# Agent attention into a gated convolution: two of five shifted taps left to DMA, three copied by VectorE, and the score and value units gathered in five blocks per batch

## The chip, the cores and the metric

The kernel runs on one core of a Trainium2 chip. The core has five engines, each with its own queue of instructions worked off in order: TensorE (PE; its weight loads are shown as PEld), VectorE (DVE), ScalarE (ACT), GpSimd (POOL) and SyncE (SP), which here issues nearly all DMA transfers. They meet through semaphores. The metric is the device time of one execution in microseconds, as the median of several runs.

## The reference

There are four batches of 12800 rows with 128 columns. Forty-nine agents first gather the values by attention over the keys, and then hand them out by attention over the queries. The result x goes through a causal convolution of five taps, whose sigmoid gates x @ w_val, and through w_out.

```python
def sm(a, b):
    s = scale * (a @ b.transpose(0, 2, 1))
    s = s - s.max(-1, keepdims=True)
    e = np.exp(s)
    return e / (e.sum(-1, keepdims=True) + 1e-09)
agent_v = sm(agents, k) @ v
x = sm(q, agents) @ agent_v
...
for k in range(K):                      # K = 5, xp is x behind K - 1 rows of zeros
    gate_pre += conv_w[k][None, None, :] * xp[:, k:k + S, :]
gate = 1.0 / (1.0 + np.exp(-gate_pre))
out = gate * (x @ w_val) @ w_out
```

## The kernel before, in words

x is never formed. Since x is (query weights) @ agent_v, the convolution, w_val and agent_v are folded per batch into small matrices (`fold_weights`), and what the matmuls move is the transposed query weights: 49 agents on the partitions, rows of the sequence in the free dimension.

**Units and chunks.** Keys, values and queries come in units of 1280 rows, ten per batch and kind. A key unit (k) is a score matmul group (sc, 16 matmuls), a copy to ks and a maximum; a value unit (v) is two exponentials, a 32x32 block transpose on VectorE (eT) and ten small matmuls (av); a query unit (q) is a score group, a VectorE transpose (sT), a maximum, and the softmax over VectorE, GpSimd and ScalarE, which ends in the tile pt. The output is worked off in 100 chunks of 512 rows, 25 per batch: six gate matmuls, two value matmuls, tanh (th, ScalarE), h = (th + 1) * val (VectorE), hh (ScalarE, 16 bits), hl = h - hh (GpSimd), and, two chunks later, three output matmuls and the scaled copy ob. The gate and the value sums have one PSUM bank each, so h of a chunk has to have read val before the next chunk's value matmuls write it.

**Precision by doubled rows.** Query weights are split in two 16-bit halves, high and low. A transposed tile x1 has 128 partitions: 49 high rows, 49 low rows, and 30 high rows a second time, which meet the low halves of the folded weights. For the other 19 agents a second tile x2 holds the high rows of all five taps (20 rows for each, 100 in all), each shifted by its tap, so that one more gate matmul (L832) and one more value matmul (L859) do for them. pt is brought into x1 by a DMA transpose (L743, all units but the first four, which go over TensorE), and x2 is filled from x1 by five shifted DMA transfers per pair of units (`shifts`, L791), or per unit for the first four. All of these but two are in SyncE's queue, between loads and stores.

**Order.** `Plan` collects the steps with their engine, an assumed duration, and what they read and write, and `order()` places them by list scheduling: TensorE's steps keep the order in which they were added, the steps of the other engines go by the longest tail of work behind them. For a transfer it assumes the wire time and a landing of 1.4 us (`LAND`). The order in which units come between chunks is a list: the tuple `at` names ten chunks of a batch, and ahead of each stand its query unit and its key or value units. Keys of the next batch come first, then the key maxima (behind chunks 7 and 8), then the values, then the fold behind chunks 20 to 24.

```python
at = (0, 2, 5, 7, 10, 12, 15, 17, 20, 22)
...
    before[t0 + at[i]].append(("q", g // NU, g % NU))
    ...
    before[t0 + at[n // part]].append(("k", b + 1, u))
    ...
    before[t0 + at[AV0 + u // 2]].append(("v", b + 1, u))
```

Loads have eleven buffers and are issued in the order of use.

Of the kernel before, what the change touches and what calls it, by code (L numbers as in the profile page):

```python
# [9 lines left out]
F32 = mybir.dt.float32  # L10
# [3 lines left out]
ALU = mybir.AluOpType  # L14
AX = mybir.AxisListType
# [16 lines left out]
X2LO = 29  # L32
X2R = 20
# [18 lines left out]
T_AT = 7  # L52
HOP = 0.09
# [9 lines left out]
class Plan:  # L63
# [7 lines left out]
    def __init__(self):  # L71
        self.steps, self.urge = [], []
        self.wrote, self.read = {}, {}

    def add(self, engine, us, fn, reads=(), writes=(), moved=0.0, key=None, urge=0.0):
# [11 lines left out]
        self.urge.append(urge)  # L87

    def order(self):
# [32 lines left out]
        while done < n:  # L122
# [33 lines left out]
            if moved:  # L156
                wire = max(wire, when + 0.5) + moved
                end = max(wire, when + us) + LAND
                lanes = lanes[1:] + [end]
# [12 lines left out]
def tile_agent_attention_gated_conv(  # L172
# [11 lines left out]
    A = 49  # L184
    NU = N // UNIT
# [26 lines left out]
    qw = ring(3, [P, NBLK, A], F32, "qw")  # L212
# [52 lines left out]
    for t in wst_sb:  # L265
        nc.gpsimd.memset(t[:, TAPS + 1 :, :], 0.0)

# [6 lines left out]
    def weights():  # L274
# [4 lines left out]
        else:  # L279
# [51 lines left out]
            for fn in ops:  # L331
# [5 lines left out]
                out=cmax, in_=conv_sb, axis=AX.X, op=ALU.max, apply_absolute_value=True  # L337
# [41 lines left out]
    def key_scores(b, u):  # L379
# [13 lines left out]
        if not first:  # L393
# [5 lines left out]
                out=kmx[b % 2][:, u, :], in_=src, axis=AX.X, op=ALU.max  # L399
# [6 lines left out]
    def key_max(b):  # L406
# [6 lines left out]
                out=m2, in_=kmx[x].rearrange("p u j -> p j u"), axis=AX.X, op=ALU.max  # L413
# [9 lines left out]
        def spread():  # L423
            nc.vector.tensor_reduce(
                out=mrow, in_=p1[0:2, 0:P].rearrange("j (g a) -> j a g", g=G),
                axis=AX.X, op=ALU.max,
# [58 lines left out]
    def fold_weights(b):  # L485
# [19 lines left out]
        def normalise():  # L505
            dve.tensor_scalar_add(den, pt[:, 0:A], 1e-9)
            dve.reciprocal(out=den, in_=den)
            dve.tensor_tensor(out=avT, in0=pt[:, AP_ : AP_ + A], in1=den, op=ALU.mult)
# [11 lines left out]
        def gate_scale():  # L520
            dve.tensor_reduce(
                out=mx[:, 0:1], in_=avT, axis=AX.X, op=ALU.max, apply_absolute_value=True
# [18 lines left out]
        x2g = wst[:, TAPS + 1, 0 : TAPS * X2R].rearrange("p (k r) -> p k r", k=TAPS)  # L541
        x2v = wst[:, TAPS + 2, 0 : TAPS * X2R].rearrange("p (k r) -> p k r", k=TAPS)
        ghi = wst[:, 0:TAPS, 0:A]
        vhi = wst[:, TAPS, 0:A]
        off = NDUP - X2LO

# [6 lines left out]
        def val_weights():  # L553
            dve.tensor_reduce(
                out=mx[:, 1:2], in_=pv[:, 0:A], axis=AX.X, op=ALU.max,
# [8 lines left out]
            rest(wst[:, TAPS, 2 * A :], pv[:, 0:NDUP], 1, vhi[:, 0:NDUP])  # L564
            rest(x2v[:, HALO, off:], pv[:, NDUP:A], 1, vhi[:, NDUP:])
# [4 lines left out]
        def gate_rest():  # L570
            rest(wst[:, 0:TAPS, 2 * A :], gw[:, :, 0:NDUP], 0, ghi[:, :, 0:NDUP])
            rest(x2g[:, :, off:], gw[:, :, NDUP:], 0, ghi[:, :, NDUP:])
# [3 lines left out]
        add("dve", 1.2, val_weights, [at_v], [(*w_, "v"), "mxv"])  # L576
        add(
            "act", 0.4,
            lambda: nc.scalar.copy(out=wst[:, 0:TAPS, A : 2 * A], in_=ghi),
# [3 lines left out]
            "act", 0.22, lambda: nc.scalar.copy(out=wst[:, TAPS, A : 2 * A], in_=vhi),  # L583
            [(*w_, "v")], [(*w_, "e")],
        )
        add("dve", 0.7, gate_rest, ["gw", (*w_, "g")], [(*w_, "r")])
# [46 lines left out]
        def split():  # L633
            dve.tensor_reduce(
                out=oscale, in_=po[:, 0:P], axis=AX.X, op=ALU.max, apply_absolute_value=True
# [31 lines left out]
    def queries(b, u):  # L667
# [6 lines left out]
        sa = sT[:, :, 0:A]  # L674
# [4 lines left out]
            lambda: nc.vector.tensor_reduce(out=qmx[x], in_=sa, axis=AX.X, op=ALU.max),  # L679
# [5 lines left out]
                out=d, in0=sa, in1=qmx[x].unsqueeze(2).to_broadcast([P, NBLK, A]),  # L685
# [10 lines left out]
        def sums():  # L696
            nc.vector.tensor_reduce(out=sm, in_=e, axis=AX.X, op=ALU.add)
# [9 lines left out]
                out=w, in0=e, in1=r.unsqueeze(2).to_broadcast([P, NBLK, A]), op=ALU.mult  # L707
# [5 lines left out]
            "act", 0.58, lambda: nc.scalar.copy(out=pt[:, :, 0:A], in_=w),  # L713
# [5 lines left out]
                out=pt[:, :, 2 * A :], in0=w[:, :, 0:NDUP], scalar1=1.0, scalar2=0.0,  # L719
# [338 lines left out]
```

## Time and profile before

| what | value |
|---|---|
| median of 3 runs | 430.09 us (429.39 to 432.08) |
| the profiled execution | 431.22 us, span 429.4 us |
| granted TensorE clock, mean | 0.996 |
| TensorE busy | 402.9 us (94%) |
| VectorE, ScalarE, GpSimd busy | 297.0, 300.4, 224.3 us |
| DMA | 128.07 MB, mean 298 GB/s |

The profile is of one execution. A row of a group of instructions gives the line, the engine, the operation, what it writes and reads, a count, then the busy time and the mean ns of one, and the idle time ahead of it with what ended most of it. A row of waits gives who waited, for whom, the us in total, how often, and the longest. The chain of waits is followed back from the last instruction; its rows are the start, the length and the work. Matmuls are pipelined and the profile models their ends, so the spacing of their starts says more than their durations.

### The profile page before, as it was taken

The page shows a single profiled execution, that of the slowest core. Times are in us where ns is not written, and L with a number is a line of the kernel's source. Part 1 is how long each engine was busy: PE and PEld are TensorE (multiplying, and loading weights), DVE is VectorE, ACT ScalarE, POOL GpSimd, SP SyncE. Part 2 cuts the span into 40 slices and gives each one's busy share as a digit, 9 for nine tenths or more (in the row PEclk, how much of TensorE's full clock was granted, in tenths as well). Part 3 has the DMA queues.
Part 4 walks back from the last instruction along what each step waited for, and adds up shares of the span by engine and source line. Part 5 has one row for each costly group of instructions (what it writes and reads, how often), then busy time and mean ns, then how long its engine had stood idle before and what let it go on. Part 6 is the DMA issues. An engine that isn't in the chain of part 4 may idle for free.

```text
span 429.4 us, 8968 instructions
## 1 busy us (share of the span) xinstructions
PE 402.9 (94%) x3307; PEld 194.8 (45%) x3307; DVE 297.0 (69%) x555; ACT 300.4 (70%) x520; POOL 224.3 (52%) x239
## 2 busy tenths in 40 slices
PE   3978888999999999999999999999999999999995
PEld 1357333345565444444555544445555544434443
DVE  3776879886786877578666887678666787566231
ACT  1464536678976577778876676778876577777875
POOL 1002246564466665544557665553356466687553
PEclk9999989999999999999999999999999999999999
DMA  8999999999999999999999999999999999887743
GB/s 288 422 415 415 371 350 337 297 285 309 343 358 294 249 270 289 307 309 305 340 329 356 292 323 292 320 312 334 306 330 257 289 291 287 215 199 173 192 156 122
DMA packets 76158, 128.07 MB, mean 298 GB/s; under 512 B 51644, under 2 KB 51900, under 8 KB 76116
## 3 DMA queue, kind: packets, MB, share of 16 engines
q1 hardware_dynamic: 76056, 127.41, 96.0%
q8 instruction: 26, 0.43, 0.4%
q14 instruction: 16, 0.13, 0.1%
q10 hardware_dynamic: 60, 0.10, 0.1%
HBM read 79.25 MB, written 26.21 MB: 246 GB/s over the span
## 4 chain that ended last, share of the span: by engine, by line
PE 65%; DMA 13%; DVE 12%; ACT 5%; issue 3%; SPq 1%; POOL 1%; DVEq 0%; ACTq 0%; POOLq 0%
PE gate L828 20%; PE sc L363 13%; PE av L463 6%; PE gate L832 4%; PE val L855 4%; PE val L859 4%; PE out L898 4%; PE out L899 4%; PE out L900 4%; DMA ld<-qT 3%; DMA ld<-vP 3%; DVE h L868 2%; ACT e L455 2%; DMA ld<-kT 2%; DMA outT<-ob 2%
## 5 line engine op out<-in xcount | busy, mean ns | idle before, releaser
L879 POOL TENSOR_TENSOR hl<-h,hh 128x512 f16<-128x512 f32 (+1 forms) x101 | 117.0, 1160 | 121.3 <-ACT hh L874 113.7
L828 PE MATMUL gate<-x,stat 128*128 128x512 f16 (+1 forms) x500 | 124.4, 378 | 2.4 <-ACT th L841 2.3
L868 DVE SCALAR_TENSOR_TENSOR h<-th,val 128x512 f32<-128x512 f32 x100 | 67.7, 677 | 69.1 <-PE out L899 46.1
L363 PE MATMUL sc<-ld,ag_sb 128*32 128x320 f32 x1280 | 102.0, 452 | 10.0 <-DMA ld<-kT 8.0
L912 ACT ACTIVATE ob<-out,oscale 128x512 f32<-128x512 f32 x98 | 67.2, 686 | 23.5 <-PE out L900 17.4
L841 ACT ACTIVATE th<-gate,unscale 128x512 f32<-128x512 f32 x100 | 68.3, 683 | 19.7 <-PE gate L832 18.0
L828 PEld LDWEIGHTS <-stat 128*128 128x128 f16 x505 | 45.6, 97 | 66.4 <-issue 19.0
L874 ACT CAST hh<-h 128x512 f16<-128x512 f32 (+1 forms) x101 | 61.4, 608 | 13.1 <-DVE h L868 12.4
L684 POOL TENSOR_TENSOR qw<-sT,qmx 128x490 f32<-128x490 f32 x40 | 41.5, 1038 | 50.2 <-DVE qmx L679 50.1
L363 PEld LDWEIGHTS sc<-ld,ag_sb 128*32 128x32 f32 x1280 | 37.0, 112 | 62.8 <-issue 22.5
L463 PE MATMUL av<-ld,eT 128*64 128x129 f32 x800 | 49.5, 275 | 1.7 <-DMA ld<-vP 1.4
L389 ACT COPY ks<-sc 128x640 f32<-128x640 f32 x40 | 27.7, 691 | 32.7 <-PE sc L363 30.6
L463 PEld LDWEIGHTS av<-ld,eT 128*64 128x64 f32 x800 | 43.7, 136 | 11.7 <-issue 7.3
L726 POOL TENSOR_TENSOR pt<-qw,pt 128x490 f16<-128x490 f32 x40 | 44.7, 1119 | 3.8 <-ACT pt L713 3.1
L455 ACT ACTIVATE e<-ks,kbias 128x320 f32<-128x320 f32 x80 | 39.0, 553 | 6.1 <-DVE kbias L444 3.3
L373 DVE STREAM_TRANSPOSE eT<-e 128x640 f32<-128x640 f32 x40 | 33.6, 842 | 11.4 <-ACT e L455 5.9
L373 DVE STREAM_TRANSPOSE sT<-sc 128x640 f32<-128x640 f32 x40 | 33.3, 834 | 10.8 <-PE sc L363 10.6
L398 DVE TENSOR_REDUCE kmx<-ks 128x2 f32<-128x640 f32 x39 | 31.4, 817 | 11.8 <-ACT ks L389 11.8
L832 PE MATMUL gate<-x,stat 100*128 100x512 f16 x100 | 38.0, 380 | 0.8 <-DMA x<-x 0.8
L855 PE MATMUL val<-x,stat 128*128 128x512 f16 x100 | 37.8, 378 | 0.1
L859 PE MATMUL val<-x,stat 100*128 100x512 f16 x100 | 37.8, 378 | 0.0
L898 PE MATMUL out<-hh,wo 128*128 128x512 f16 x98 | 37.1, 379 | 0.0
(125 smaller groups left out, 392.1 us busy)
## 6 DMA issues: line engine op xcount, KB each, us to landing
ld<-vP SPq DMA_DIRECT2D x40, 645.0 KB
ld<-kT SPq DMA_DIRECT2D x40, 640.0 KB
ld<-qT SPq DMA_DIRECT2D x40, 640.0 KB
outT<-ob SPq DMA_DIRECT2D x48, 512.0 KB
x<-x SPq DMA_DIRECT2D x90, 100.0 KB
x<-x SPq DMA_DIRECT2D x18, 50.0 KB
outT<-ob SPq DMA_DIRECT2D x3, 256.0 KB
x<-pt SPq DMA_TRANSPOSE x36
```

The source lines that it names most:

```text
L363: nc.tensor.matmul(out=out[g * BLK : (g + 1) * BLK, j, 0:GT], lhsT=ag_sb[:, b, j * BLK : (j + 1) * BLK], rhs=src[:, g * GT : (g + 1) * GT] ...
L373: nc.vector.transpose(out=out.rearrange("p n (j i) -> p j n i", j=2), in_=in_.rearrange("p j (n i) -> p j n i", i=BLK),)
L463: nc.tensor.matmul(out=av[o : o + AP_, 0 : C + 1], lhsT=et[:, n, :], rhs=vt[:, n, :], start=(u == 0 and n < 2), stop=(u == NU - 1 and n >= ...
L828: nc.tensor.matmul(out=pg, lhsT=stat[:, k, :], rhs=x1[:, c : c + w], start=(k == 0), stop=False,)
L832: nc.tensor.matmul(out=pg, lhsT=stat[0 : TAPS * X2R, TAPS + 1, :], rhs=x2[0 : TAPS * X2R, o2 : o2 + w], start=False, stop=True,)
L841: lambda: nc.scalar.activation(out=th, in_=pg, func=AF.Tanh, scale=unscale[:, 0:1]),
L855: nc.tensor.matmul(out=pv, lhsT=stat[:, TAPS, :], rhs=x1[:, PAD + n0 : PAD + n0 + w], start=True, stop=False,)
L859: nc.tensor.matmul(out=pv, lhsT=stat[0 : TAPS * X2R, TAPS + 2, :], rhs=x2[0 : TAPS * X2R, o2 : o2 + w], start=False, stop=True,)
L868: lambda: nc.vector.scalar_tensor_tensor(out=h, in0=th, scalar=1.0, in1=pv, op0=ALU.add, op1=ALU.mult),
L874: "act", 0.16 + 0.42 * scale, lambda: nc.scalar.copy(out=hh, in_=h),
L879: lambda: nc.gpsimd.tensor_tensor(out=hl, in0=h, in1=hh, op=ALU.subtract),
L912: lambda: nc.scalar.activation(out=ob[:, o : o + w], in_=po, func=AF.Copy, scale=oscale),
```

## The change

Two things are changed. First, of the five shifted copies into x2, taps 0, 2 and 4 are now VectorE copies (`tensor_copy`, within SBUF, 16 bits) and taps 1 and 3 stay DMA transfers. The rows are laid out anew, so that the copies read and write from partitions that are multiples of 32: pt has two of the doubled rows ahead of the high rows (`A0 = 2`), the 19 rows that x2 needs begin at partition 32 of x1, and taps 0, 4 and 2 lie at partitions 0, 64 and 32 of x2. Tap 1 has its rows at 97, and tap 3 what is left, in two pieces (at 116 and 20). The unused rows of x2 are set to zero once, on GpSimd, and the matmuls over x2 read all 128 partitions. The agents are laid out with the two extra columns on the host, so that scores and the query softmax are 51 wide instead of 49 where they must be. The small operations that fill the low halves of the folded weights (`rest`) follow the new rows: three on the value side where two stood, six on the gate's where two stood. `Plan.add` has a new number, `spare`, which lets the plan count 2 us more for the landing of a DMA transpose.

Second, `at` names five chunks twice each: a block of two query and four key or value units ahead of chunks 0, 5, 10, 15 and 20.

```diff
+SPARE = 2
...
+X2_ROWS = (
+    ((0, 19, 0),),
+    ((0, 19, 97),),
+    ((0, 19, 32),),
+    ((0, 12, 116), (12, 7, 20)),
+    ((0, 19, 64),),
+)
...
+    for t in x2s:
+        nc.gpsimd.memset(t, 0.0)
...
-                [(*p_, n) for n in range(3)], [("x1", u)], 2.4,
+                [(*p_, n) for n in range(3)], [("x1", u)], 2.4, spare=SPARE,
...
         for k in range(TAPS):
             c = PAD - HALO + u0 * UNIT + k
-
-            q, e = (nc.scalar, "act") if g == 0 and k % 2 else (nc.sync, "dma")
-            add(
-                e, 0.75,
-                lambda k=k, c=c, q=q: q.dma_start(
-                    out=x2[k * X2R : (k + 1) * X2R, o : o + n * UNIT],
-                    in_=x1[X2LO : X2LO + X2R, c : c + n * UNIT],
-                ),
-                src, [("x2", s % 3, o + i * UNIT, k) for i in range(n)], 0.26 * n,
-            )
+            for i, m, r in X2_ROWS[k]:
+                out, in_ = x2[r : r + m, o : o + w], x1[REST + i : REST + i + m, c : c + w]
+                keys = [("x2", s % 3, o + j * UNIT, k, i) for j in range(n)]
+                if k % 2 == 0:
+                    add(
+                        "dve", 0.08 + 0.33 * n,
+                        lambda out=out, in_=in_: nc.vector.tensor_copy(out=out, in_=in_),
+                        src, keys,
+                    )
+                    continue
...
+                add(
+                    e, 0.75, lambda out=out, in_=in_, q=q: q.dma_start(out=out, in_=in_),
+                    src, keys, 0.013 * m * n,
+                )
...
-    at = (0, 2, 5, 7, 10, 12, 15, 17, 20, 22)
+    at = (0, 0, 5, 5, 10, 10, 15, 15, 20, 20)
```

What moves on TensorE, at chunk 35 (ten chunks into the second batch): its rows before, where L363 is a score unit, L463 a value unit, L828 the first gate matmul of a chunk and L900 the last output matmul; numbers behind names tell buffers apart.

```order
L900 MATMUL out<-hl_113,wo_123 128x512
L363 MATMUL sc_128<-ld_70,ag_sb 32x320 x8
L463 MATMUL av<-ld_71,eT_83 64x129 x10
L463 MATMUL av<-ld_61,eT_84 64x129 x10
L828 LDWEIGHTS stat_121
L828 MATMUL gate<-x_99,stat_121 128x512
...
L363 MATMUL sc_129<-ld_62,ag_sb 32x320 x8
L463 MATMUL av<-ld_63,eT_82 64x129 x10
L463 MATMUL av<-ld_64,eT_83 64x129 x10
```

The same place after; the lines have other numbers (L379 score, L479 value, L870 gate, L942 output).

```order
L942 MATMUL out<-hl_113,wo_123 128x512
L379 MATMUL sc_128<-ld_70,ag_sb 32x320 x8
L379 MATMUL sc_129<-ld_71,ag_sb 32x320 x8
L479 MATMUL av<-ld_61,eT_83 64x129 x10
L479 MATMUL av<-ld_62,eT_84 64x129 x10
L479 MATMUL av<-ld_63,eT_82 64x129 x10
L479 MATMUL av<-ld_64,eT_83 64x129 x10
L870 LDWEIGHTS stat_121
L870 MATMUL gate<-x_99,stat_121 128x512
```

Two score units and four value units now stand together ahead of chunk 35, and the block that stood ahead of chunk 37 is gone from there.

On VectorE, the rows before around the h of the chunks at the same place (h is L868, the transposes of value and query units are L373, the maximum over the agents L679).

```order
L868 SCALAR_TENSOR_TENSOR h_107<-th_104,val 128x512
L373 STREAM_TRANSPOSE sT_86<-sc_128 128x2x10x32
L679 TENSOR_REDUCE qmx_88<-sT_86 128x10
L373 STREAM_TRANSPOSE eT_84<-e_80 128x2x10x32
L373 STREAM_TRANSPOSE eT_82<-e_81 128x2x10x32
L373 STREAM_TRANSPOSE eT_83<-e_80 128x2x10x32
L868 SCALAR_TENSOR_TENSOR h_108<-th_105,val 128x512
L868 SCALAR_TENSOR_TENSOR h_106<-th_103,val 128x512
```

And after, with what each row waits for (L910 is h, L389 the transposes, L821 the new copies; DMAHW is a transfer's landing).

```order
L910 SCALAR_TENSOR_TENSOR h_107<-th_104,val 128x512 [waits Activation_49,Pool_49]
L389 STREAM_TRANSPOSE eT_82<-e_81 128x2x10x32 [waits DVE_49,PE_49]
L389 STREAM_TRANSPOSE sT_85<-sc_129 128x2x10x32 [waits Pool_49]
L389 STREAM_TRANSPOSE eT_83<-e_80 128x2x10x32 [waits DVE_49,PE_49,Activation_49]
L389 STREAM_TRANSPOSE eT_84<-e_81 128x2x10x32 [waits DVE_49,PE_49,Activation_49]
L389 STREAM_TRANSPOSE eT_82<-e_80 128x2x10x32 [waits DVE_49,PE_49,Activation_49]
L821 COPY x_102<-x_99 19x2560 [waits DMAHW5_49,DMAHW4_49]
L910 SCALAR_TENSOR_TENSOR h_108<-th_105,val 128x512 [waits PE_49,Activation_49]
L821 COPY x_102<-x_99 19x2560 x2
L910 SCALAR_TENSOR_TENSOR h_106<-th_103,val 128x512 [waits PE_49,Activation_49,Pool_49]
```

Three copies have come in around two h, and the first of them waits for the two DMA transposes of its pair of units; the h behind it is behind that wait as well.

More of the change, by code (lines that the diff above doesn't have):

```diff
@@ L87, in add @@
         self.urge.append(urge)
+        self.spare.append(spare)
     def order(self):
@@ L820, in gates @@
         xs = [("x1", u) for u in units] + [("x1b", u) for u in units]
-        x2k = [("x2", segs_[0] % 3, h, k) for h in halves for k in range(TAPS)]
+        x2k = [
+            ("x2", segs_[0] % 3, h, k, i) for h in halves for k in range(TAPS)
+            for i, _, _ in X2_ROWS[k]
+        ]
         st = [("stat", x, 0), ("stat", x, 1)]
@@ L832, in matmuls @@
             nc.tensor.matmul(
-                out=pg, lhsT=stat[0 : TAPS * X2R, TAPS + 1, :],
-                rhs=x2[0 : TAPS * X2R, o2 : o2 + w], start=False, stop=True,
+                out=pg, lhsT=stat[:, TAPS + 1, :], rhs=x2[:, o2 : o2 + w],
+                start=False, stop=True,
             )
@@ L859, in matmuls @@
             nc.tensor.matmul(
-                out=pv, lhsT=stat[0 : TAPS * X2R, TAPS + 2, :],
-                rhs=x2[0 : TAPS * X2R, o2 : o2 + w], start=False, stop=True,
+                out=pv, lhsT=stat[:, TAPS + 2, :], rhs=x2[:, o2 : o2 + w],
+                start=False, stop=True,
             )
```

100 lines of the change are left out of this document (61 added, 39 removed).

## The prediction

> **What bounds the kernel now.** The busy totals of the page come first, then the windows, which give every engine's busy time in each stage.
>
> ```profile
> PE 402.9 (94%) x3307; PEld 194.8 (45%) x3307; DVE 297.0 (69%) x555; ACT 300.4 (70%) x520; POOL 224.3 (52%) x239
> ```
>
> ```profile
> core 0: us, PE busy (x) PEld busy (x) DVE busy (x) ACT busy (x) POOL busy (x), PEclk, DMA share, GB/s
> 0.00:50.30 50.30, 37.28 (x483) 21.80 (x484) 32.66 (x74) 23.61 (x42) 6.62 (x17) 1.00 0.98 381
> 50.30:100.00 49.70, 45.28 (x379) 18.80 (x377) 42.01 (x78) 32.02 (x55) 27.02 (x30) 0.97 1.00 324
> 100.00:150.00 50.00, 49.21 (x442) 26.52 (x438) 37.13 (x69) 37.38 (x68) 30.96 (x32) 1.00 0.99 311
> 150.00:200.00 50.00, 49.91 (x402) 22.18 (x400) 36.64 (x67) 37.23 (x63) 25.77 (x28) 1.00 1.06 298
> 200.00:250.00 50.00, 48.90 (x424) 25.67 (x421) 36.61 (x69) 37.11 (x67) 30.36 (x32) 1.00 1.01 323
> 250.00:300.00 50.00, 49.96 (x405) 22.33 (x404) 36.54 (x67) 38.00 (x65) 26.29 (x27) 1.00 1.03 316
> 300.00:350.00 50.00, 48.73 (x399) 25.57 (x398) 35.91 (x66) 35.98 (x65) 28.92 (x31) 1.00 1.08 298
> 350.00:421.00 71.00, 69.84 (x374) 29.95 (x372) 38.62 (x70) 54.61 (x91) 45.89 (x44) 1.00 0.76 201
> ```
>
> From 100 us on TensorE is busy 49 to 50 of every 50 us: it is the bound there, and only its own work or its idle time can shorten the span. From the first gate chunk (50.3 us) to 421 us the PE column adds up to 361.8 of 370.7 us, so 8.9 us are idle, 4.4 of them in the stage up to 100 us, where VectorE has 42.0 of 49.7 us filled. The DMA share is about 1 almost throughout, but what matters is who waits for it. The waits of TensorE, first from 100 to 421 us, then from 50.3 to 100 us:
>
> ```profile
> PE gate L828 <- ACT th L841: 1.6, 5, 0.6
> PE sc L363 <- DVE sT L373: 1.6, 2, 0.8
> PE gate L832 <- DMA x<-x: 0.8, 1, 0.8
> ```
>
> ```profile
> PE val L655 <- DVE wsp L642: 1.9, 1, 1.9
> PE sc L757 <- POOL pt L726: 1.2, 1, 1.2
> ```
>
> The shifted taps, which the change takes from the DMA queue, cost TensorE 0.8 us, once. So the first half of the change has little to win directly. The second half works on TensorE's row of work; the chain of waits, in order of time, shows what that is worth.
>
> ```profile
> 115.06 1.08 PE gate L828 x5
> 116.14 0.22 PE gate L832
> ...
> 117.44 1.21 PE sc L363 x16
> 118.65 2.35 PE av L463 x40
> 121.01 1.19 PE gate L828 x5
> ```
>
> ```profile
> 158.00 3.47 PE sc L363 x48
> ```
>
> Five gate matmuls take 1.08 us behind a chunk and 1.19 behind a block of units. One score unit (x16) takes 1.21 alone; three take 3.47, so a further one costs 1.13.
>
> **Fewer blocks.** TensorE's program has 39 stretches of unit matmuls before and 23 now (counted over its rows in order). Each one saved is worth 0.11 (gate) and 0.08 (score): 16 x 0.19 = **-3.0 us**, on the engine that sets the end. With the gate's part alone it is -1.8. The value pairs are put at nothing: 2.35 for two is the same pace inside a longer run.
>
> **The copies' price.** No 16-bit SBUF-to-SBUF copy stands in the trace. The nearest rows:
>
> ```profile
> L868 DVE SCALAR_TENSOR_TENSOR h<-th,val x100: 422/687/690, 52.5 to 422.3; 128x512 f32<-128x512 f32 x99, 128x256 f32<-128x256 f32 x1
> ```
>
> ```profile
> L604 DVE COPY stat<-av 128x512 f16<-128x512 f16 x3 | 1.3, 418 | 0.1
> L316 DVE TENSOR_SCALAR ob<-ob 128x261 f32<-128x261 int32 x1 | 0.3, 296 | 0.0
> L548 DVE SCALAR_TENSOR_TENSOR wst<-av,rs,wst 128x19 f16<-128x19 f32 x3 | 0.7, 227 | 0.0
> L879 POOL TENSOR_TENSOR hl<-h,hh 128x512 f16<-128x512 f32 x99 | 115.6, 1169 | 120.4 <-ACT hh L874 112.7 <-DMA x<-x 3.9 <-DMA x<-pt 3.0
> ```
>
> h at 256 and 512 elements (422, 687 ns) gives 1.04 ns per element and 157 ns fixed. With that fixed part the 16-bit copy from PSUM runs at (418-157)/512 = 0.51, and the 4-byte one-input operation within SBUF at (296-157)/261 = 0.53: each halves the price for its own reason. A tap copy is both. If the halvings multiply, 2560 elements take 0.157 + 2560 x 0.26 = 0.82 us and 1280 take 0.49; if not, 1.49 and 0.82. I take the low end, because the copy shares the property of each row. There are 18 pairs of units and 4 single ones, three copies each: 54 x 0.82 + 12 x 0.49 = **50 us** of VectorE (90 at the high end), 297 to about 347.
>
> The Trainium skill, "VectorE: DVE Perf Modes", section "The perf-mode tier table", gives 693 ns for a 2048-element 16-bit copy in SBUF, its fastest tier; an estimate from that page, with its 150 fixed cycles, is also 0.82 us. No run here shows it yet.
>
> **What of it lies on the path.** Per 50 us between 100 and 350: two and a half pairs, 7.5 x 0.82 = 6.2 us, some 0.2 for rows that are 510 wide instead of 490, and 0.6 for the fold: VectorE goes from 36.6 to 43.6, 87%. Ten-microsecond windows that are already that full:
>
> ```profile
> 120.00:130.00 10.00, 10.00 (x101) 5.72 (x96) 8.67 (x16) 6.80 (x13) 6.88 (x9) 1.00 1.12 338
> 220.00:230.00 10.00, 10.00 (x91) 5.32 (x88) 8.29 (x16) 6.03 (x11) 5.60 (x6) 1.00 1.10 360
> 240.00:250.00 10.00, 9.21 (x79) 4.37 (x78) 8.84 (x25) 6.71 (x12) 6.58 (x9) 1.00 1.02 325
> ```
>
> Away from a batch's turn VectorE at 83 to 87% costs TensorE nothing; at the turn (240) it loses 0.8. The cover is TensorE's own work: h has to be ready before the next chunk's value matmuls, that is within three output and six gate matmuls. At 0.217 each (six lie between 116.14 and 117.44) these are 1.95 us, of which h takes 0.69, so 1.26 are to spare. I put **+0.5 us** here, between -1.6 (the waits for sT go, since keys come two chunks earlier) and what the rivals say.
>
> From 50.3 to 100 us VectorE has 7.7 us free and gets 9 x 0.49 + 3 x 0.82 = 6.9 us of copies, and two more key units come early. All 6.9 may reach the path; or the early units fill TensorE's idle 4.4 and something is won (-1). I take **+1.0**: the free time is just enough, and the two waits shown there, 1.9 and 1.2, are the kind that grow.
>
> The fold has five more VectorE operations (one on the value side, four on the gate's), each at most some 19 columns or a few: 5 x 0.23 = 1.1 us. In batch 0 that lies on the path, with VectorE's weights in front of TensorE's transposes:
>
> ```profile
> 46.61 0.69 DVE wst L548 x3
> 47.30 0.14 issue
> 47.43 0.61 PE gate L593 x8
> ```
>
> **+1.1 us**; in the other three batches chunks cover it. The three memsets of x2 go on GpSimd at the start, where it is busy 6.6 of 50.3 us: nothing.
>
> **What goes from the queue.** Five transfers per segment become three, two of them smaller. The chain at the last batch turn:
>
> ```profile
> 325.44 7.18 DMA x<-pt
> ...
> 332.69 0.76 SPq L791
> ...
> 335.77 5.16 DMA x<-x
> ```
>
> The first tap is issued at 332.69 and the last lands at 340.93. Two issues fewer at some 0.75 each bring the landing 1.5 us forward, more than the 0.8 that TensorE waited: **-0.8**. Taps 1 and 3 still go by DMA, so the 5.16 stays.
>
> Sum: -3.0 + 0.5 + 1.0 + 1.1 - 0.8 = -1.2 us. The profiled execution took 431.22 (span 429.4 and 1.8 around it), so 430.0 against it; the median of the runs is 1.1 below that execution, so **428.9 us**. With the better ends (-1.6 and -1 for +0.5 and +1.0) the sum is -5.3, 424.8 us; with the worse ones (-1.8 for the blocks, the whole 6.9) it is +5.9, 436.0.
>
> **Rival 1: the stalls shrink.** Keys are done by block 5 instead of 7, and SyncE issues 44 transfers fewer. If half of the 8.9 us idle goes and the copies hide, -3.0 + 1.1 - 4.4 = -6.3: 423.8. For it: the waits are for VectorE and ScalarE work that comes in pieces now merged. Against it: VectorE only gets fuller. Chance 0.28.
>
> **Rival 2: VectorE stands waiting for the transposes.** The taps waited on SyncE before; now the first copy of a pair waits in VectorE's queue, and behind it stand h and the transposes of the same block.
>
> ```profile
> SPq L791 <- DMA x<-pt: 26.1, 15, 3.9
> ```
>
> SyncE stood 26.1 us, 15 times: 1.74 each. If a copy's place in the queue is as early as its transfer's was, 1.74 - 1.26 = 0.48 us reach TensorE 18 times: +8.6, and 437.5 us. It decides from 1.26 us a pair. Against it: the plan now counts 2 us more for a landing, and the copies lie by blocks of units, where h is not pressing. Chance 0.15.
>
> **Rival 3: VectorE and GpSimd hold each other up.** Two VectorE operations with two SBUF inputs (minimum, median, maximum):
>
> ```profile
> L698 DVE SCALAR_TENSOR_TENSOR qsm<-qsm,tiny x40: 170/171/974, 34.4 to 392.7; 128x10 f32<-128x10 f32 x40
> L706 DVE TENSOR_TENSOR qw<-qw,qr x40: 628/670/1512, 35.4 to 393.2; 128x490 f32<-128x490 f32 x40
> ```
>
> Some take 0.80 and 0.84 us more than the median, less than one GpSimd operation (1.17). If copies do this too and, three in a row, each waits for a whole operation, 7.5 x 1.17 = 8.8 us come on top of 43.6 per 50: 2.4 over, in five such stretches +12, and 440.9 us. It decides from (50 - 43.6)/7.5 = 0.85 us per copy; with copies of 1.49 us VectorE has 48.6 filled already, and 0.2 us decides. Against it: the medians are the minimum or near it, so most operations meet nothing, and GpSimd is busy half the time. Chance 0.12.
>
> The Trainium skill, "SBUF — State Buffer", section "Who interferes with whom", states this as a rule that speaks against the change: VectorE's two-port modes and GpSimd share one port pair as an exclusive lock, and whoever comes second stands until the other is done. By that rule the stretched rows are such meetings, and the trace agrees, the excess staying under GpSimd's 1.17 us.
>
> **The numbers.** 0.45 for the sum, 0.28, 0.15, 0.12 for the rivals; 428.9 is the likeliest case. The range, 421 to 438, takes in rival 1 with some room and rival 2, and leaves most of rival 3 out. A measurement can tell about 1%, 4.3 us, from no change. Faster by more: rival 1 and 0.02 of the sum, 0.30. Within: 0.41 of the sum. Slower: rivals 2 and 3 and 0.02 of the sum, 0.29.
>
> **What would show it.** Copies of 2560 near 0.82 us with a maximum under 2; VectorE near 350 us busy; gate groups of 1.19 us in 16 places fewer; TensorE idle after 100 us still near 4.5. Rival 2 would show as VectorE waiting for x<-pt, rival 3 as a copy's mean well over its minimum. I am wrong if TensorE's idle time moves by more than 5 us either way, or the copies take 1.49.

## The result, and the profile after

The changed kernel takes 449.38 us (median of 4 runs, 447.89 to 451.44), the kernel before 431.08 in the same session: a ratio of 1.043, 95% interval 1.037 to 1.049. It is 18 us slower, where I had forecast 428.9 us and a range that ended at 438.

The busy totals of the changed kernel and, below them, its chain by engine; then the chain by engine of the kernel before.

```profile
PE 403.1 (90%) x3307; PEld 198.2 (44%) x3307; DVE 373.5 (84%) x641; ACT 301.7 (68%) x520; POOL 246.1 (55%) x242
...
PE 47%; DVE 25%; DMA 12%; issue 7%; ACT 4%; POOL 3%; SPq 1%; DVEq 0%; ACTq 0%; POOLq 0%
```

```profile
PE 65%; DMA 13%; DVE 12%; ACT 5%; issue 3%; SPq 1%; POOL 1%; DVEq 0%; ACTq 0%; POOLq 0%
```

TensorE is busy as long as before (403.1 us against 402.9) in a span of 445.5 us against 429.4, so by these totals the loss is idle time. VectorE is the engine that grew, by 76 us, and its share of the chain doubled. GpSimd grew by 22, of which 6.6 are the three memsets. By stage (columns as in the prediction's windows):

```profile
100.00:150.00 50.00, 47.03 (x440) 25.96 (x433) 45.39 (x70) 36.09 (x65) 31.68 (x30) 1.00 1.02 279
150.00:200.00 50.00, 46.27 (x346) 19.98 (x346) 45.76 (x83) 33.92 (x57) 26.51 (x27) 1.00 0.98 304
200.00:250.00 50.00, 47.68 (x438) 26.22 (x439) 44.76 (x68) 37.71 (x69) 32.81 (x32) 1.00 1.01 304
250.00:300.00 50.00, 46.40 (x371) 20.52 (x364) 43.51 (x81) 33.71 (x57) 25.70 (x25) 1.00 0.90 285
```

Before, TensorE lost 0.0 to 1.1 us in these windows; now it loses 2.3 to 3.7 in each, and VectorE is filled 43.5 to 45.8 us instead of 36.5 to 37.1. The loss has no one place. The waits over the whole span, and the copies' own row (minimum, median, maximum) with the one wait ahead of them:

```profile
ACT hh L916 <- DVE h L910: 41.7, 48, 2.8
PE val L897 <- DVE h L910: 10.0, 14, 2.4
PE gate L874 <- DMA x<-x: 2.3, 1, 2.3
```

```profile
L821 DVE COPY x<-x x66: 481/819/1801, 41.2 to 423.9; 19x2560 f16<-19x2560 f16 x54, 19x1280 f16<-19x1280 f16 x12
...
  DMA x<-pt: 0.5, 1
```

ScalarE waits for h 41.7 us (12.4 before), and TensorE waits for it with the next value matmuls, a wait that no row of before showed. Its one wait for a shifted tap is longer too, 2.3 us where it was 0.8. The undisturbed copy takes 819 ns, the 0.82 us I had worked out, but some take up to 1801. What happens there is seen in the timeline around 138 us (start, length, engine and work):

```profile
138.00 0.69 DVE L910 SCALAR_TENSOR_TENSOR h<-th,val 128x512 f32<-128x512 f32 x1 [1.23 <-ACT th L883]
...
138.72 4.16 DVE L821 COPY x<-x 19x2560 f16<-19x2560 f16 x3
138.80 1.69 POOL L752 TENSOR_TENSOR pt<-qw,pt 128x490 f16<-128x490 f32 x1
...
139.52 0.69 ACT L883 ACTIVATE th<-gate,unscale 128x512 f32<-128x512 f32 x1
...
140.45 1.74 POOL L921 TENSOR_TENSOR hl<-h,hh 128x512 f16<-128x512 f32 x1
...
142.91 0.69 DVE L910 SCALAR_TENSOR_TENSOR h<-th,val 128x512 f32<-128x512 f32 x1
```

Three copies take 4.16 us in place of 2.46. GpSimd's two operations beside them take 1.69 and 1.74 us; in the prediction's row the second kind has a mean of 1.17. The chunk's th is ready at 140.21, and its h starts at 142.91, 2.7 us later, more than the 1.26 us I had counted as spare.

### The profile page after: what moved, and what is told of

It reads as the page before. It is cut to its first block, busy times and chain, and to the rows that moved or that the text cites. A ratio compares the mean times of both kernels' runs of the same rounds, so it can differ in the third digit from the quotient of the medians.

```text
span 445.5 us, 9048 instructions
## 1 busy us (share of the span) xinstructions
PE 403.1 (90%) x3307; PEld 198.2 (44%) x3307; DVE 373.5 (84%) x641; ACT 301.7 (68%) x520; POOL 246.1 (55%) x242
## 4 chain that ended last, share of the span: by engine, by line
PE 47%; DVE 25%; DMA 12%; issue 7%; ACT 4%; POOL 3%; SPq 1%; DVEq 0%; ACTq 0%; POOLq 0%
PE gate L870 12%; PE sc L379 12%; DVE h L910 7%; DVE x L821 6%; PE av L479 6%; DMA ld<-vP 5%; DMA ld<-qT 3%; PE val L897 3%; PE out L941 3%; PE out L940 3%; PE val L901 3%; PE out L942 2%; PE gate L874 2%; DVE sT L389 2%; ACT th L883 2%
## 5 line engine op out<-in xcount | busy, mean ns | idle before, releaser
L921 POOL TENSOR_TENSOR hl<-h,hh 128x512 f16<-128x512 f32 (+1 forms) x101 | 123.5, 1224 | 121.2 <-ACT hh L916 119.3
L870 PE MATMUL gate<-x,stat 128*128 128x512 f16 (+1 forms) x500 | 125.1, 380 | 0.9 <-ACT th L883 0.9
L379 PE MATMUL sc<-ld,ag_sb 128*32 128x320 f32 x1280 | 98.0, 450 | 12.0 <-DMA ld<-kT 7.8
L910 DVE SCALAR_TENSOR_TENSOR h<-th,val 128x512 f32<-128x512 f32 x100 | 67.8, 678 | 29.2 <-PE out L941 16.6
L916 ACT CAST hh<-h 128x512 f16<-128x512 f32 (+1 forms) x101 | 61.6, 610 | 41.8 <-DVE h L910 41.7
L883 ACT ACTIVATE th<-gate,unscale 128x512 f32<-128x512 f32 x100 | 68.3, 683 | 18.3 <-PE gate L874 17.2
L954 ACT ACTIVATE ob<-out,oscale 128x512 f32<-128x512 f32 x98 | 67.2, 686 | 12.8 <-PE out L942 11.7
L870 PEld LDWEIGHTS <-stat 128*128 128x128 f16 x505 | 47.2, 98 | 64.0 <-issue 14.2
L821 DVE COPY x<-x 19x2560 f16<-19x2560 f16 (+1 forms) x66 | 69.4, 1052 | 2.4 <-DMA x<-pt 0.5
L379 PEld LDWEIGHTS sc<-ld,ag_sb 128*32 128x32 f32 x1280 | 38.4, 112 | 61.9 <-issue 18.9
L710 POOL TENSOR_TENSOR qw<-sT,qmx 128x510 f32<-128x510 f32 x40 | 43.7, 1097 | 37.8 <-DVE qmx L705 37.8
L752 POOL TENSOR_TENSOR pt<-qw,pt 128x490 f16<-128x490 f32 x40 | 50.0, 1252 | 3.4 <-ACT pt L739 3.2
L479 PE MATMUL av<-ld,eT 128*64 128x129 f32 x800 | 48.1, 276 | 1.0 <-DVE qsm L724 0.3
L479 PEld LDWEIGHTS av<-ld,eT 128*64 128x64 f32 x800 | 44.4, 137 | 7.7 <-issue 3.6
L897 PE MATMUL val<-x,stat 128*128 128x512 f16 x100 | 37.7, 377 | 10.8 <-DVE h L910 10.0
L389 DVE STREAM_TRANSPOSE eT<-e 128x640 f32<-128x640 f32 x40 | 33.5, 839 | 9.3 <-ACT e L471 6.7
L874 PE MATMUL gate<-x,stat 128*128 128x512 f16 x100 | 37.9, 379 | 2.3 <-DMA x<-x 2.3
L901 PE MATMUL val<-x,stat 128*128 128x512 f16 x100 | 37.7, 377 | 0.0
L940 PE MATMUL out<-hh,wo 128*128 128x512 f16 x98 | 37.1, 379 | 0.0
L942 PE MATMUL out<-hl,wo 128*128 128x512 f16 x98 | 37.1, 379 | 0.0
```

Of the source, the lines that this page charges most:

```text
L379: nc.tensor.matmul(out=out[g * BLK : (g + 1) * BLK, j, 0:GT], lhsT=ag_sb[:, b, j * BLK : (j + 1) * BLK], rhs=src[:, g * GT : (g + 1) * GT] ...
L479: nc.tensor.matmul(out=av[o : o + AP_, 0 : C + 1], lhsT=et[:, n, :], rhs=vt[:, n, :], start=(u == 0 and n < 2), stop=(u == NU - 1 and n >= ...
L821: lambda out=out, in_=in_: nc.vector.tensor_copy(out=out, in_=in_),
L870: nc.tensor.matmul(out=pg, lhsT=stat[:, k, :], rhs=x1[:, c : c + w], start=(k == 0), stop=False,)
L883: lambda: nc.scalar.activation(out=th, in_=pg, func=AF.Tanh, scale=unscale[:, 0:1]),
L897: nc.tensor.matmul(out=pv, lhsT=stat[:, TAPS, :], rhs=x1[:, PAD + n0 : PAD + n0 + w], start=True, stop=False,)
```

## The experiments

All ratios are to the kernel before, run beside each.

### VectorE's time, with the same program around it

Four kernels differ from the changed one in one instruction: a maximum, or a copy of every 160th element, stands in the place of each copy. So the rows of taps 0, 2 and 4 in x2 are not filled; everything else, the order too, is as changed.

```diff
-  nc.vector.tensor_copy(out=out, in_=in_)
+  nc.vector.tensor_reduce(out=out[:, 0:1], in_=in_[:, ::4], axis=AXIS, op=ALU.max)    # e3_no_port
+  nc.vector.tensor_reduce(out=out[:, 0:1], in_=in_[:, ::160], axis=AXIS, op=ALU.max)  # e4_short
+  nc.vector.tensor_copy(out=out[:, ::160], in_=in_[:, ::160])                         # e12_port_only
+  nc.vector.tensor_reduce(out=out[:, 0:1], in_=in_[:, : w * 19 // 25 : 2], ...)       # e13_long_no_port
```

> The changed kernel, but each VectorE copy of a tap is replaced by a maximum over every fourth element of the same rows: 640 elements (320 for a single unit), which by the maxima of the query path takes about 0.82 us (0.49), written to one column. Taps 0, 2 and 4 are left out of x2 by this; the waits, the place in the queue and the plan stay. Theory A1 (the meetings of copies with GpSimd on a shared port): a maximum has one SBUF input, does not wait for GpSimd, takes 0.82 at its median and its mean alike, VectorE is some 20 us less busy, and the time falls to 434 to 440 us. Theory A2 (the plain time of the copies on VectorE): the time stays within 3 us of the changed kernel.

> As the run without the port, but the maximum goes over 16 elements (8 for a single unit), some 0.17 us; taps 0, 2 and 4 are left out of x2. What is left is the order of the queue, the wait of a pair's first operation for the DMA transposes, and the small operations of the fold. Theory A (time of the copies on VectorE, by themselves or by the port): 424 to 430 us. Rival (the wait for the transposes in VectorE's queue, or the order of its rows): 438 us or more.

> The changed kernel, but each tap copy takes only every 160th element, 16 (8 for a single unit): the form of the copy without its time; the rest of taps 0, 2 and 4 is left out of x2. Theory A1 (copies and GpSimd stop each other): these take about 0.17 us alone, their longest over 0.9, their mean 0.3 or more over the minimum, and the time lies 3 to 8 us above the run with short maxima, 432 to 437. If such a short copy does not meet GpSimd, mean and minimum agree and the time is that of the short maxima, 427 to 431.

> The changed kernel with each copy replaced by a maximum over 973 (single units: 486) elements of the same rows, so x2's three even taps are not filled. By the maxima over 640 elements (0.81 us) and 16 (0.17 us) it should take some 1.15 us, the mean that the copies took, and VectorE should be busy some 372 us as with the copies (373.5); but no copy stands behind GpSimd and GpSimd not behind a copy (its busy time some 233 us, not 246). Theory L (only VectorE's filled time counts, whoever fills it): 447 to 450 us. Theory M (the meetings also cost through GpSimd's longer operations, and through the unlucky copy that takes 1.8 us): 438 to 443 us.

The row of that instruction in each, in the order e4, e12, e3, e13:

```profile
L821 DVE TENSOR_REDUCE x<-x x66: 155/171/175, 41.3 to 406.8; 19x1 f16<-19x16 f16 x54, 19x1 f16<-19x8 f16 x12
```

```profile
L821 DVE COPY x<-x x66: 174/194/1176, 42.6 to 403.8; 19x16 f16<-19x16 f16 x54, 19x8 f16<-19x8 f16 x12
```

```profile
L821 DVE TENSOR_REDUCE x<-x x66: 476/812/843, 41.6 to 411.9; 19x1 f16<-19x640 f16 x54, 19x1 f16<-19x320 f16 x12
```

```profile
L821 DVE TENSOR_REDUCE x<-x x66: 649/1158/1161, 42.1 to 423.7; 19x1 f16<-19x973 f16 x54, 19x1 f16<-19x486 f16 x12
```

A maximum never takes much longer than its median; a copy does, even one of 16 elements (194 ns, up to 1176). So copies meet GpSimd and maxima don't. This is the rule of the Trainium skill, "SBUF — State Buffer", section "Who interferes with whom", which exempts the reduction on this chip; the rows agree. What it costs:

| in the copy's place | VectorE busy | GpSimd busy | median us | ratio (95%) |
|---|---|---|---|---|
| 16-element maximum (e4) | 317.8 | 232.3 | 428.57 | 0.994 (0.991 to 0.998) |
| 16-element copy (e12) | 333.0 | 232.8 | 428.55 | 0.994 (0.991 to 0.997) |
| maximum as long as an undisturbed copy (e3) | 353.8 | 233.0 | 435.93 | 1.011 (1.006 to 1.017) |
| maximum as long as the copies' mean (e13) | 374.3 | 233.0 | 448.76 | 1.040 (1.036 to 1.045) |
| the copy (the change) | 373.5 | 246.1 | 449.38 | 1.043 (1.037 to 1.049) |

Two comparisons settle what the meetings do. From e4 to e12 they add 15 us to VectorE and nothing to the time. From e13 to the change they come in at equal VectorE time, with 13 us more on GpSimd, and the time differs by 0.6 us, inside both intervals. So the meetings cost what they add to VectorE's time and nothing beside it: 0.33 us a copy (1.148, the mean of the 2560-element copies, less 0.82). From e4 on, the first 15 us of added VectorE time are free, the next 21 go with 7.4 us, the next 20 with 12.8 to 13.5.

Not all of the 7.4 us is VectorE's. Both executions of e3 had a mean granted TensorE clock of 0.983, and in its trace the ten microseconds from 110 us on are granted 0.77; e12 shows 1.00 there (third figure from the end; e3 first).

```profile
110.00:120.00 10.00, 10.00 (x37) 4.02 (x36) 4.80 (x9) 5.87 (x10) 5.28 (x6) 0.77 1.07 283
```

```profile
110.00:120.00 10.00, 10.00 (x66) 4.45 (x68) 7.00 (x14) 8.62 (x16) 6.30 (x7) 1.00 1.01 262
```

Two of e4's eight executions had the same 0.983 and took 431.15 and 431.52 us, so at a like clock the maxima of e3 cost 4.4 to 4.8 us. The step from e3 to e13, whose executions had 0.986 to 0.991, is then some 3 us larger than 12.8; this is an estimate.

Is it the filled time or the row of three operations that h stands behind? In e4 a maximum over 400 elements that nobody reads was put behind every h: as much VectorE time as in e13, in a hundred short pieces.

```diff
+  nc.vector.tensor_reduce(out=junk, in_=h[:, 0 : min(w, 400)], axis=AXIS, op=ALU.max)   # behind each h
```

> The changed kernel with each copy replaced by a maximum over 16 elements (0.17 us, as in the run with short maxima, 428.6 us; x2's three even taps are not filled), and behind every h on VectorE a maximum over 400 of its elements (some 0.56 us) that nobody reads. VectorE is then busy some 374 us, as in the run with long maxima (374.3 us, 448.8 us), but in 100 pieces of 0.56 us, one per chunk, none ahead of its own h, instead of rows of three in a row of 3.5 us. If it is VectorE's share of filled time that costs: 446 to 452 us. If it is the length of the row of copies in which an h stands and waits (over the 1.26 us to spare): 428 to 433 us. In between, both.

```profile
PE 406.8 (90%) x3307; PEld 198.3 (44%) x3307; DVE 376.5 (83%) x742; ACT 301.3 (66%) x520; POOL 233.5 (52%) x242
...
L916 DVE TENSOR_REDUCE junk<-h 128x1 f32<-128x400 f32 (+1 forms) x101 | 57.3, 567 | 3.5
```

454.79 us, ratio 1.055 (1.052 to 1.058): above what either reading expected, and far from the 428 to 433 of the row-length reading. VectorE's added time costs in pieces of 0.57 us too. The fill of VectorE from 50 to 400 us doesn't give the price by itself, though. The sums of the windows (busy us of 350), in the order before, e12, e3, e13, e17:

```profile
sum 350.00, PE 341.13 PEld 161.41 DVE 257.61 ACT 256.17 POOL 205.03; mean PE 48.73 PEld 23.06 DVE 36.80 ACT 36.60 POOL 29.29
```

```profile
sum 350.00, PE 339.20 PEld 165.92 DVE 290.59 ACT 260.69 POOL 208.75; mean PE 48.46 PEld 23.70 DVE 41.51 ACT 37.24 POOL 29.82
```

```profile
sum 350.00, PE 337.33 PEld 164.01 DVE 305.63 ACT 255.66 POOL 204.78; mean PE 48.19 PEld 23.43 DVE 43.66 ACT 36.52 POOL 29.25
```

```profile
sum 350.00, PE 330.39 PEld 159.39 DVE 316.02 ACT 248.24 POOL 197.26; mean PE 47.20 PEld 22.77 DVE 45.15 ACT 35.46 POOL 28.18
```

```profile
sum 350.00, PE 324.67 PEld 156.56 DVE 306.10 ACT 240.34 POOL 191.67; mean PE 46.38 PEld 22.37 DVE 43.73 ACT 34.33 POOL 27.38
```

e3 and e17 show the same 87% of VectorE, e3 with TensorE at 48.2 of 50 and e17 at 46.4. A stretched stage lowers the share that its own work shows, so a busy share read afterwards is not the load that was asked. Where the work lies may count as well: e17 puts it into every chunk, also around the fold, where TensorE's transposes now wait 6.3 us for VectorE's weights (2.8 in e13). How much of the 6 us between e17 and e13 that explains is not shown.

One more kernel lets the plan count what the copies really take, in case it only ordered them badly:

```diff
-                        "dve", 0.08 + 0.33 * n,
+                        "dve", 0.09 + 0.53 * n,
```

> The changed kernel, whole, in which the plan counts 1.15 us for a copy of a pair and 0.62 for one unit, as measured, in place of 0.74 and 0.41; only the order of the queues moves. Theory P (the copies stand ahead of h because the plan holds them too cheap): 440 to 445 us. Theory A (VectorE's time and the meetings with GpSimd, wherever the copies stand): 446 to 452 us.

451.74 us, ratio 1.048 (1.042 to 1.053). The plan's price was not the cause.

### The blocks, and what stands in SyncE's queue

`at` was changed alone (e1); the copies were put in with the old `at` (e2), as were the 16-element maxima (e5); then key and value units alone went by five blocks (e8), and query units alone (e9).

```diff
-    at = (0, 2, 5, 7, 10, 12, 15, 17, 20, 22)
+    at = (0, 0, 5, 5, 10, 10, 15, 15, 20, 20)      # e1 on the kernel before; e2 and e5 the other way round
...
+    atu = (0, 0, 5, 5, 10, 10, 15, 15, 20, 20)     # e8: for k and v alone; e9: the same for q
```

> Only the table of blocks is changed (five blocks of two query and four key or value units); the five shifted taps stay DMA transfers. Theory A (the copies on VectorE are what cost the 18 us): the merged blocks are worth their 16 x 0.19 us and nothing is lost, 425 to 429 us, faster than before or the same. Theory B (the bursts of six units starve the chunks): most of the loss is here, 440 us or more. With both at work it lies between, 432 to 440.

> The changed kernel with the old table of ten blocks; taps 0, 2 and 4 are VectorE copies. Theory A: the loss stays, and the 3 us of the merged blocks go too, 447 to 453 us. Theory B: close to before, 428 to 434 us.

> The run with short maxima (taps 0, 2 and 4 left out of x2, 16 elements instead of a copy) with the old table of ten blocks. It asks what it is worth to have three of five taps off the DMA queue when VectorE pays nearly nothing for it. Theory Q (the queue of SyncE costs the ten blocks too): as far below before as the short run lies below the blocks alone, 422 to 426 us. Theory R (the taps only hurt the merged blocks): 428 to 432 us, the same as before.

> The kernel before with the key and value units in five blocks of four and the query units left one by one at ten chunks. Theory Bq (in the merged blocks it is the second query unit that hurts, since its work on VectorE and GpSimd comes at once with the first's): 427 to 431 us, no loss. Theory Bk (the four key or value units in a row starve the chunks): 433 to 438 us, as with all units merged.

> The kernel before with the query units in five blocks of two and the key and value units at the ten chunks as before: the complement of the run with key and value blocks. Theory Bk (four key or value units in a row are what costs): 427 to 431 us, no loss. If both halves hurt, 433 us or more.

The blocks alone are slower than before: 435.68 us, 1.012 (1.007 to 1.018). Key and value units alone give 436.97 (1.014, 1.008 to 1.020). Query units alone have a median of 434.97, but their four executions fall apart into 429.99 and 432.46 on one side and 437.48 and 438.78 on the other, so a loss by them is not shown. In e1 one wait of ScalarE stands out:

```profile
ACT ob L912 <- DMA outT<-ob: 16.6, 6, 4.4
```

```profile
215.21 7.43 DMA outT<-ob
```

ScalarE can't write the next output tile ob while its buffer, one of three, is still being stored; before, this cost 4.1 us. The stores stand in SyncE's queue among loads and taps, and the second fence, a piece of e1's chain, shows one that lands 7.43 us after its issue. One store in the chain of before takes 7.25 us, so what is new is that ScalarE stands for stores six times instead of twice. If that is the cause, more buffers give the time back:

```diff
-NOB = 3
+NOB = 5
```

> The kernel before with five merged blocks and five output buffers instead of three. In the run with blocks only, ScalarE waited 16.6 us, 6 times, for stores before it could write an output buffer (none of that length in before). Theory S (stores held up in SyncE's queue behind transposes, taps and loads of the merged blocks): 428 to 432 us. Theory W (the work of the units on VectorE and GpSimd, which comes in bursts, makes h and hl late): 434 to 438 us, as with three buffers.

> The kernel before with five output buffers instead of three, and ten blocks as they stood. If the gain of the five blocks with five buffers (427.8 us) is the buffers' alone: 428 us. If it is the blocks' shorter program on TensorE (my -3.0, once the stores hold nothing up): 430.5 to 431.5 us, as before, since the kernel before waited only 4.1 us for stores, twice.

> The changed kernel with five output buffers. If the two costs add up (held-up stores of the merged blocks some 8 us, VectorE's copies some 19): 441 to 442 us. If VectorE's filled time alone is what ends last, as the ten-block version with copies (447.4) suggests: 446 to 449 us.

| | ten blocks | five blocks |
|---|---|---|
| taps by DMA, 3 buffers | 430.5 to 431.3 (medians of before) | 435.7 (e1) |
| taps by DMA, 5 buffers | 431.0 to 439.1 (e14) | 427.8 (e10) |
| 16-element maxima for three taps, 3 buffers | 430.0 (e5) | 428.6 (e4) |
| copies, 3 buffers | 447.4 (e2) | 449.4 (the change) |
| copies, 5 buffers | | 451.0 (e15) |

With five buffers the blocks are worth something: e10 takes 427.81 us, ratio 0.992 (0.989 to 0.995), the lowest median of all, and lower than that of both kernels. It waits 4.0 us for stores; GpSimd's wait for transposes to leave pt, 7.1 us in e1, is gone too. The buffers alone don't do it. The executions of e14 fall apart into one at 430.99 us, the profiled one, and five at 437.55 to 439.09, none of them under the kernel before; why more buffers should slow the ten blocks is open, since no trace caught it. Times of 437 to 439 us also come up in e9, and single ones of 436 to 437 us in the kernel before, so something that is in no trace here may act in these as well. With the copies in, the buffers don't help: e15 is at 450.98, and neither its waits nor those of the changed kernel show ScalarE waiting for stores. So what e10 wins can't be added to the change.

Without the copies' VectorE time (e5), taking three taps off the queue is worth 1.1 us at ten blocks (ratio 0.997, 0.994 to 0.999). In five blocks it is 7 us (e1 to e4), and e4 doesn't show the store waits. The layout and the plan's longer landing are in both differences.

### The new layout with all taps by DMA

To have the layout without VectorE, all five taps were left to transfers, first with the 19 rows that the copies use (e7; the changed kernel's own transfers have 20, 12 and 8 rows), then with even numbers of rows, 20, 12 and 8 (e11), both with ten blocks. And in the kernel before one tap's 20 rows were issued as 12 and 8, six transfers instead of five (e16).

```diff
-                if k % 2 == 0:
+                if False:
...
+                if m % 2 and (k % 2 == 0 or r == 20):      # e11 only
+                    m += 1
...
+PIECES = ((0, 0, 20), (1, 0, 20), (2, 0, 20), (3, 0, 12), (3, 12, 8), (4, 0, 20))      # e16, on the kernel before
```

> The changed kernel with all five taps as DMA transfers (taps 0, 2 and 4 of 19 rows) and the old ten blocks: what is left of the change is the layout, that is rows 51 wide, the memsets, five more operations in each fold, six transfers per segment instead of five, and the 2 us that the plan adds to a landing. All theories so far: 1 us of fold and nothing else, 430 to 434 us. If the layout is dearer than that, 436 us or more, the price of the copies is smaller than the run with copies only made it look.

> The layout control again, ten blocks and all taps by DMA, with taps 0, 2 and 4 and the second piece of tap 3 as 20 and 8 rows instead of 19 and 7 (one row more is brought along). If the odd number of rows made the transfers three times as long, this takes 430 to 435 us; if not, it stays near 600.

> The kernel before with the fourth tap's transfer of 20 rows issued as two, of 12 and 8 rows: six transfers per segment, the same bytes, everything else as it was. If one transfer more on SyncE's queue is what made the all-transfer version of the new layout slow (443.5): 440 to 444 us, TensorE waiting some 10 us more for x<-x. If the layout itself or the plan's longer landing did it: 431 to 433 us.

e7 takes 604.26 us, 1.402 (1.397 to 1.407), e11 443.51, 1.028 (1.024 to 1.033), e16 438.72, 1.020 (1.012 to 1.028). From e7, the wait of TensorE for taps, a piece of the chain, the line of GB/s in 40 slices of 104 to 125 us, and the queue from 115 to 123 us (packets, MB, share of the 16 DMA engines' time):

```profile
PE gate L874 <- DMA x<-x: 127.9, 20, 11.8
...
107.64 14.61 DMA x<-x
...
GB/s 492 372 423 462 423 373 462 461 308 419 322 88 39 310 400 318 84 32 181 86 54 20 29 29 20 29 29 29 20 29 29 20 29 27 23 31 45 290 282 281
...
q1 hardware_dynamic: 47, 0.21, 6.4%
```

From 115 to 123 us, while the chain waits for the taps, all DMA engines together move 20 to 31 GB/s; the tap lands 14.61 us after its issue, and the 20-row tap in the chain of before took 5.16. The Trainium skill, "DMA: Bandwidth & Descriptors", section "Why a DMA increments its semaphore by 16 and not by 1", says that a transfer goes over as many of the 16 engines as the largest number up to 16 that divides the row counts: by this, 10 for 20 rows and one for 19. The trace agrees for 19: 6.4% is about one sixteenth, the time of one engine. In e11 even rows cure that, and yet it is 12 us over before; TensorE's matmuls wait for x<-x 6.7 us there (0.8 before). e16, with only the sixth transfer added, doesn't wait so. From its waits:

```profile
ACT ob L913 <- DMA outT<-ob: 12.6, 6, 4.5
PE gate L829 <- ACT th L842: 9.2, 11, 2.2
```

One transfer more per segment, of no more bytes, goes with 8 us more and with late stores, as the merged blocks do; ScalarE waits 7.8 us for transposes besides (0.6 before). More buffers were not tried here, so that the stores are the cause is read off this one trace. It doesn't carry over to e11, which has the sixth transfer too: ScalarE waits for stores only 5.1 us there (4.1 before). What makes its taps late is open.

## Why the prediction was wrong

**The bound** was read rightly: TensorE, idle 8.9 us of 370. That made the first half of the change worth little, and so it is: with the copies' time taken out, e4 stands at 428.57. My sum without its two terms for the copies was -3.0 + 1.1 - 0.8 = -2.7 us, 428.4 against the 431.08 of the kernel before. That the two agree so closely is luck, since the blocks, the fold and the queue each did something else than their terms say, as told below.

**The path cost of the copies, +0.5 and +1.0, is the step that failed.** I had the size of the undisturbed copy right (0.82 worked out, 0.819 measured), and with maxima of just that length in the copies' place, as e3 has, the time is 7.4 us over e4 (4.4 to 4.8 at a like clock), not 1.5. The reasoning was that windows of before with VectorE at 83 to 87% cost TensorE nothing. Those were peaks of 10 us between emptier windows. My reading is that late work could be made up there, and that an average of 87% over 350 us has nowhere to make it up; no run tests that reading by itself. What is measured is that the knee lies between e12 (83% from 50 to 400 us, no cost) and e3 (87%, 4.4 to 7.4 us).

**The copies' mean** was the second error: 1.148 us, not 0.82. The 20 us that meetings with GpSimd add to VectorE's time cost 12.8 to 13.5 us more, since they come on top of the knee. Together: -2.5 (e4) + 7.4 + 13.4 = +18.3, with some 3 us of the 7.4 put down to the clock.

**Rival 3** named this mechanism, at 0.12 and 440.9 us. Its mechanism holds, VectorE's copies and GpSimd stand for each other; the two stretched rows that it rested on are of operations with two inputs from SBUF, and that copies do the same is shown by e12 beside e4. Its sizes don't: a copy waits 0.33 us on average, not 1.17, and the path cost doesn't begin where VectorE's row is over-full (50 of 50) but between 83 and 87%. By its own sum, 43.6 + 7.5 x 0.33 = 46.1 of 50, nothing would have been lost: the waiting stayed far under its threshold of 0.85 us a copy, and the time was lost even so.

**Fewer blocks, -3.0.** TensorE's work did get shorter, by more than that: it is busy 402.9 us before, and 398.1 and 398.2 in e1 and e10. In the changed kernel it is 403.1 all the same, though the rows of the units are shorter there too; what lengthens the rest is not shown. These rows in the changed kernel and before:

```profile
L379 PE MATMUL sc<-ld,ag_sb 128*32 128x320 f32 x1280 | 98.0, 450 | 12.0 <-DMA ld<-kT 7.8 <-DVE sT L389 4.2
L479 PE MATMUL av<-ld,eT 128*64 128x129 f32 x800 | 48.1, 276 | 1.0 <-DVE qsm L724 0.3 <-DVE qw L732 0.3 <-DMA ld<-vP 0.3
```

```profile
L363 PE MATMUL sc<-ld,ag_sb 128*32 128x320 f32 x1280 | 102.0, 452 | 10.0 <-DMA ld<-kT 8.0 <-DVE sT L373 1.9
L463 PE MATMUL av<-ld,eT 128*64 128x129 f32 x800 | 49.5, 275 | 1.7 <-DMA ld<-vP 1.4 <-DVE eT L373 0.3
```

4.0 us less on scores (I had 16 x 0.08 = 1.3) and 1.4 on the value units, which I had put at nothing; the gate's row has no gain (124.4 before, 125.1 after), where I had 1.8. But this reaches the time only where nothing else waits: -3.5 us in e10 against before (with the buffers), -1.4 from e5 to e4 (whose intervals overlap), +4.8 in e1 (stores), +2.0 from e2 to the change (VectorE). That merged blocks bunch the stores behind loads and taps was in none of my cases.

**The fold, +1.1**, was sized too high for the five operations. Before, the transposes of the folded weights waited 1.1 us for VectorE, in batch 0 alone; after:

```profile
PE av L619 <- DVE wst L561: 2.7, 3, 1.1
PE gate L619 <- DVE wst L561: 1.4, 1, 1.4
```

That is 0.3 us more in batch 0, and 2.7 in the three batches that I thought covered by chunks. The 2.7 are not the five operations': e5, which has them at ten blocks, shows only the 1.4, and e1 and e10, which don't have them, wait 1.0 and 1.8 us in later batches. They come with the merged blocks and a fuller VectorE.

**The queue, -0.8**: e5, in which all else of the change but the blocks and the copies' time stands too, is 1.1 us faster than before. But the wait that I had priced didn't go. TensorE waits for x<-x 1.8 us in e5, 3.4 in e4 and 2.3 in the changed kernel, once each, where it was 0.8.

**Rival 2** is refuted: VectorE waited for x<-pt once, 0.5 us. The copies' place in VectorE's queue is late enough. **Rival 1**, shrinking stalls, is not seen in the changed kernel. **The memsets** at nothing: no run takes them out alone, but in the trace what they hold up on VectorE (below) is made up by 14.89 us, where VectorE writes moe_sb (14.88 before).

## What to carry to other kernels

An engine that is free a quarter of the time on average has less to give than that: here VectorE had 111 us free in e4 (317.8 of 429.2 us busy) and could take 15 of them at no cost; from there each further microsecond cost 0.2 to 0.35 us, then 0.6 to 0.8. Price the fill over whole stages, with what the added work does to the durations of its neighbours, and not by the fullest window that did no harm. Before merging work into larger blocks, look for what queues behind them: here the blocks paid clearly only with more output buffers.

## What the runs showed of the hardware

A maximum and a copy of equal length on VectorE are not equal beside GpSimd: 843 ns at most against 1801. The memsets of x2, three operations on GpSimd from 2.26 to 8.84 us, hold up VectorE as well. Of its six integer operations of this kind one starts at 5.04 us and takes 3949 ns, until just behind the last memset, and the others take about 300, as all six did before (minimum, median, maximum):

```profile
L282 POOL MEMSET x<- 128x2560 f16 x3 | 6.6, 2231 | 0.0
...
L307 DVE TENSOR_SCALAR ob<-ob x6: 277/298/3949, 5.0 to 13.6; 128x261 int32<-128x261 int32 x6
```

```profile
L291 DVE TENSOR_SCALAR ob<-ob x6: 288/298/299, 4.9 to 13.1; 128x261 int32<-128x261 int32 x6
```

A transfer of 19 rows used about one of the 16 DMA engines (e7). And a gap on TensorE was followed by a lower clock in some runs: in e4's windows TensorE idles 3.4 us from 100 to 110 us, where the granted clock (third figure from the end) is 0.86, and the next 10 us run at 0.80.

```profile
100.00:110.00 10.00, 6.60 (x76) 4.49 (x73) 5.83 (x13) 5.20 (x11) 3.79 (x4) 0.86 0.98 332
110.00:120.00 10.00, 10.00 (x39) 4.07 (x38) 5.14 (x10) 5.98 (x10) 5.82 (x6) 0.80 0.95 255
```

The same wait for a tap is 3.2 us in e3 and 3.0 in e15, with 0.77 and 0.83 from 110 to 120 us; in e12, e13 and the changed kernel it is 2.8, 2.4 and 2.3 us, and the clock there stays at 1.00. That the gap brings the clock down is read from this order; no run tests it.
